# Three edits to a retention and mixer kernel: how late its replay takes a DMA turn to be, which engine turns the third batch's u, and where the first batch's token mixing is added

## The chip, the cores and the metric

The kernel runs on one core of a Trainium2 chip. The metric is the device time of one execution, in microseconds (us). The engines are TensorE (PE in the profile; its weight loads are a row of their own, PEld), VectorE (DVE), ScalarE (ACT), GpSimd (POOL) and SyncE (SP). Each runs its own list of instructions in order and waits for the others through semaphores. Loads of q, k, v and of the weights are issued by POOL, DMA turns (transposes) by SP, stores of the output by ACT.

## What is computed

For 4 batches, 8 heads, 768 steps and head size 64, a decaying state is built up and read at each step, and the result goes through a mixer over tokens and a mixer over channels:

```python
for t in range(S):                                   # gamma = 1 - 2 ** (-5 - h)
    state = gamma * state + einsum('bhd,bhe->bhde', k[:, :, t], v[:, :, t])
    y[:, :, t] = scale * einsum('bhd,bhde->bhe', q[:, :, t], state)
x = y.transpose(0, 2, 1, 3).reshape(B, S, H * D)     # 4 x 768 x 512
h = relu(x^T @ w_tok1) @ w_tok2                      # 768 -> 256 -> 768, over tokens
u = x + h^T
out = u + relu(u @ w_ch1) @ w_ch2                    # 512 -> 1536 -> 512, over channels
```

## The kernel before

The recurrence is done in 6 chunks of 128 steps: within a chunk as a masked score matrix, between chunks through a state that is decayed once per chunk. Work is split into a front and a back.

`front(b, p)` handles one batch b and one pair p of heads (4 pairs, 128 columns of x). In order: k is scaled to fp16 (L408, L410); k and q are turned so that the head size lies on the partitions (kT, qT); the chunk states are formed (L467) and chained on DVE (L476, L479), then scaled (L490, L492); scores are matmuls of kT and qT (L510, two groups of 6), masked by DVE (L518); y is summed from state and scores (L532, L535); ACT or DVE scales it into X (L548, L552); POOL or DVE casts it to fp16 (L565); the first token matrix gives 256 rows (L576), which ReLU copies out as h1 (L584, L586).

Then the batches differ. For **the first batch** u is formed twice. Turned, for the channel mixer's input: L598 multiplies w_tok2 with h1, L601 adds x by an identity matrix, and the sum is copied out as uT (L608). Not turned, for the sum at the end: L627 multiplies h1 with w_tok2 (two groups of 6 matmuls a pair), and DVE adds it to X (L635); these two carry `late=0.5`, so that they stand behind the rest of that batch in priority. For **the other batches** L627 and L635 make u in X, L643 casts it to fp16, and it is turned into uT.

A turn is done in one of two ways. Below batch `XB = 2` TensorE turns k, q and u by 6 or 12 transposing matmuls into a bank (L445, L443, L664), and ACT or DVE copies it out (L452, L670). From batch `XB` on, SP issues a DMA transpose: L431 for k and q, L654 for u.

`back(b)` is the channel mixer, in two halves of 384 tokens. For each of 12 slices of 128 hidden channels 4 matmuls of 384 columns (L696) fill a bank, and ACT copies it out with ReLU into h2 (L710). For each of three blocks of 128 tokens a bank collects 12 matmuls of 512 columns (L723, six pairs); DVE adds X to it (L731), and ACT issues the store (L737).

**Banks.** The accumulator has 8 banks. The first batch's front may use banks 0 to 6, later fronts 0 to 4, every back 5 to 7. A bank is taken by the first matmul into it and is free when its last reader is done.

**The order** is made by the program itself before anything runs. `arrange()` lists operations greedily: of all whose inputs have been placed and for which a bank and buffers are to be had, it looks for those that can start first by its costs, and takes among them (within 20 ns on that engine) the one with the best priority. A front's priority is (0, b, ...), a back's (1, b, number), so a back's work goes where no front's work is ready. `replay(order)` then runs that list against a model of the DMA queues: a DMA starts to move `FIRST` ns after its issue, its rounds take as long as all queues in flight take together, and `LAND` ns later it counts as landed. What the replay gives for each DMA becomes the latency by which the next `arrange()` places it. This is repeated for some turns, and the order with the least replayed time is kept. A matmul that waits on the chip holds up all that stands behind it in TensorE's list. Early in the kernel, matmuls on zeros (L781) fill planned gaps.

The loads form one line on POOL, in order; a load is issued only when the one eight before it has landed. The lines that the prediction speaks of are L431, L510, L576, L598, L601, L608, L627, L635, L654, L664, L670, L696, L710, L723 and the tables in L51 to L79.

Of the kernel before, what the change touches and what calls it, by code (L numbers as in the profile page):

```python
# [17 lines left out]
def kernel(  # L18
# [29 lines left out]
    ctx.enter_context(tc.manual_schedule())  # L48


    BUFS = dict(kf=6, qf=6, k16=3, q16=3, v16=8, kT=4, qT=4, U=2, r16=3, am=8, X=3, x16=5, h1=5, u16=3,  # L51
                uT=3, h2=2, o=4)
    BANKS = dict(first=range(0, 7), front=range(0, 5), back=range(5, 8), fill=range(7, 8))
    SEM = 80
    XB = 2
    ops = []

    class Slot:
# [16 lines left out]
            ops.append(self)  # L75

    GEN = dict(SP=20, ACT=20)
    FIRST = dict(SP=600, POOL=1700, ACT=600)
    LAND = dict(SP=800, POOL=1000, ACT=1500)  # L79

    def replay(order):

        lines = {e: [] for e in ("PE", "ACT", "DVE", "POOL", "SP")}
        held, bank_of = {t: [] for t in BUFS}, {i: None for i in range(8)}
        before = {}
        for o in order:
# [12 lines left out]
        at = {e: 0 for e in lines}  # L99
        free = dict(PE=0, ACT=2500, DVE=0, POOL=400, SP=700)  # L100
        dmas = {e: [] for e in ("SP", "POOL", "ACT")}
        left = {e: None for e in dmas}
        gens = [0, 0, 0]
        t, dt, n = 0, 25, len(order)
        while n:
            for e, line in lines.items():
                while at[e] < len(line) and free[e] <= t:
                    o = line[at[e]]
                    at_ = free[e]
                    for d in o.deps + o.after:  # L110
                        if d.end is None:
                            at_ = None
                            break
                        if d.eng == e and d.eng == "PE":
                            continue
                        at_ = max(at_, d.end + (30 if d.eng == e and not d.dma else SEM))
                    if at_ is None or at_ > t:
                        break
                    for s in before[o]:
                        for u in s.users:  # L120
                            if u.end is None:
                                at_ = None
                                break
                            if u.eng == e and e == "PE":
                                continue
                            at_ = max(at_, u.end + SEM)
                        if at_ is None:
                            break
                    if at_ is None or at_ > t:
                        break  # L130
                    at[e] += 1
                    o.start = at_
                    free[e] = at_ + o.cost[0]
                    if o.dma:
                        if e == "SP":
                            free[e] = max(at_ + 550, gens[-2])
                            gens.append(max(at_ + 550, gens[-1]) + o.dma[0] * GEN[e])
                            o.made = gens[-1]
                        else:
                            o.made = 0  # L140
                        dmas[e].append(o)
                    else:
                        o.end = at_ + o.cost[1]
                        n -= 1
            on = []
            for e, q_ in dmas.items():
                if q_ and left[e] is None and q_[0].start + FIRST[e] <= t:
                    left[e] = float(q_[0].dma[0])
                if left[e] is not None:
                    on.append((e, q_[0]))  # L150
            round_ = sum(o.dma[1] for e, o in on)
            for e, o in on:
                step = dt / round_
                if o.made > t:
                    step = min(step, dt / GEN[e])
                left[e] -= step
                if left[e] <= 0:
                    left[e] = None
                    dmas[e].pop(0)
                    o.end = t + LAND[e]  # L160
                    n -= 1
            t += dt
            if t > 400000:
                raise RuntimeError("the order does not end")
        for o in order:
# [105 lines left out]
    def one(eng, cost, emit):  # L271
        return [(eng, cost[0], cost[1], emit)]
# [79 lines left out]
    loads, x_done, uT_done, y_done, t2_done = {}, {}, {}, {}, {}  # L352
    Xs = [Slot("X") for _ in range(B)]
    UTs = [Slot("uT") for _ in range(B)]
    first_of = {}
    rcount = [0]

    def load(b, p):
# [11 lines left out]
    def front(b, p):  # L370
# [196 lines left out]
            cast_ops.append(op(either(emit, POOL=(460, 530), DVE=(520, 560)),  # L567
                               [ev] + cast_ops, [X16] if hf == 0 else [], [X] if hf == 0 else [X, X16]))

        T1, H1 = Slot(FA), Slot("h1")  # L570

        def emit():
            acc = tile_of(T1, [P, 512], FP)
# [5 lines left out]
                [T1], [X16])  # L579

        def emit(e):
            h1 = tile_of(H1, [P, NJ, P], F16).rearrange("p j c -> p (j c)")
            if e == "ACT":
                nc.scalar.activation(h1, T1.tile[:, :NJ * P], AF.Relu)  # L584
            else:
                nc.vector.tensor_scalar(h1, T1.tile[:, :NJ * P], 0.0, None, ALU.max)  # L586
        hr = op(either(emit, ACT=act(NJ * P), DVE=dve(NJ * P)),
                [t1], [H1], [T1])

        if first:  # L590

            for hf in range(2):
                G = Slot(FA)

                def emit(hf=hf, G=G):
                    acc = tile_of(G, [P, 512], FP)
                    for jt in range(NJ):
                        nc.tensor.matmul(acc[:, :SH], H1.tile[:, jt], wt2[:, jt, hf * SH:(hf + 1) * SH],  # L598
                                         start=(jt == 0), stop=False)
                    for i in range(HC):  # L600
                        nc.tensor.matmul(acc[:, i * P:(i + 1) * P], X16.tile[:, hf * HC + i], ident16,  # L601
                                         start=False, stop=(i == HC - 1))
                g = op(one("PE", (500, 650), emit), [hr, wops["t2"], cast_ops[hf]], [G], [H1, X16])

                def emit(e, hf=hf, G=G):
                    if UT.tile is None:
# [7 lines left out]
                if opens:  # L614
                    first_of[b, "uT"] = e
                uT_done[b, p, hf] = e
        U16 = Slot("u16")
        casts = []
        for hf in range(2):
            T2 = Slot(FA)  # L620

            def emit(hf=hf, T2=T2):
                acc = tile_of(T2, [P, 512], FP)
                for i in range(HC):
                    t = slice((hf * HC + i) * P, (hf * HC + i + 1) * P)
                    for jt in range(NJ):
                        nc.tensor.matmul(acc[:, i * P:(i + 1) * P], wt2[:, jt, t], H1.tile[:, jt],  # L627
                                         start=(jt == 0), stop=(jt == NJ - 1))
            t2 = op(one("PE", (340, 500), emit), [hr, wops["t2"]], [T2], [H1], late=0.5 if first else 0)
            if not first:  # L630
                t2_done[b * NP + p] = t2

            def emit(hf=hf, T2=T2):
                xo = X.tile[:, half(hf), pc]
                nc.vector.tensor_tensor(  # L635
                    xo, xo, T2.tile[:, :HC * P].rearrange("p (i d) -> p i d", d=P), ALU.add)
            ad = op(one("DVE", (500, 560), emit), [t2, cast_ops[hf]], [], [T2, X], late=0.5 if first else 0)
            x_done[b, p, hf] = ad
            if not first:
                def emit(e, hf=hf):  # L640
                    if hf == 0:
                        tile_of(U16, [P, NC, P], F16)
                    (nc.vector if e == "DVE" else nc.gpsimd).tensor_copy(  # L643
                        U16.tile[:, half(hf)], X.tile[:, half(hf), pc])
                casts.append(op(either(emit, POOL=(460, 530), DVE=(520, 560)),
                                [ad] + casts, [U16] if hf == 0 else [], [X] if hf == 0 else [X, U16]))
        if first:
            return
        opens = (b, "uT") not in first_of
        if b >= XB:  # L650
            def emit():
                if UT.tile is None:
                    tile_of(UT, [P, NP, S], F16)
# [25 lines left out]
    def back(b):  # L679
# [6 lines left out]
        for sh in range(2):  # L686
# [28 lines left out]
            for i in range(HC):  # L715
                A, O = Slot("back"), Slot("o")
                last = None
                for f0 in range(0, NF, 2):
                    def emit(f0=f0, i=i, A=A, H2=H2):
                        if f0 == 0:  # L720
                            tile_of(A, [P, 512], FP)
                        for ft in range(f0, f0 + 2):
                            nc.tensor.matmul(A.tile, H2.tile[:, ft, i * P:(i + 1) * P],  # L723
                                             wc2[ft // FW][:, ft % FW],
                                             start=(ft == 0), stop=(ft == NF - 1))
                    last = op(one("PE", (432, 590), emit), rel[f0:f0 + 2] + [wops["c2", f0 // FW], last],
                              [A] if f0 == 0 else [], [H2] if f0 == 0 else [A, H2])

                def emit(sh=sh, i=i, A=A, O=O):
                    o = tile_of(O, [P, C], FP)  # L730
# [29 lines left out]
    for b in range(B):  # L760
        back(b)
    best = None
    for turn in range(10):
        order = arrange()
        t = replay(order)
        if best is None or t < best[0]:
# [47 lines left out]
```

## Time and profile before

| | us |
|---|---|
| median of 3 runs | 220.92 |
| lowest and highest | 220.74, 221.6 |
| the profiled execution | 222.71 |
| its span, first to last instruction | 220.9 |
| TensorE busy | 199.7 |
| ACT, DVE, POOL busy | 110.6, 101.0, 79.3 |
| mean granted clock of TensorE | 0.981 |

The page of the profile gives busy time by engine and by 40 slices of the span, the chain of work that ended last, groups of instructions by line, and DMA issues with the time until they land. Other views show the instructions in order of time, with the idle time of the engine ahead of each and what ended it, the waits by who waited for whom, and busy time and granted clock in chosen stretches. A row such as `L510 PE MATMUL bank<-qT,kT` names the line, the engine, the operation, and what it writes and reads.

### The profile page before, as it was taken

How to read it: one execution, taken by the hardware profiler on the slowest of the kernel's cores; microseconds unless marked ns; L12 is line 12 of the kernel's file. 1: busy time of each engine (PE TensorE's matmuls, PEld its weight loads, DVE VectorE, ACT ScalarE, POOL GpSimd, SP SyncE). 2: the span in 40 equal slices, each digit the busy share in tenths (PEclk: the TensorE clock that was granted, in tenths of full speed). 3: DMA queues.
4: the chain of work that ended last, by engine and by line, in shares of the span. 5: the costliest groups of instructions: out<-in, count | busy, mean ns of one | idle time of the engine just before them, and what ended most of it. 6: DMA issues, size and time to landing. Idle time of an engine off the chain costs nothing.

```text
span 220.9 us, 4774 instructions
## 1 busy us (share of the span) xinstructions
PE 199.7 (90%) x1937; PEld 122.4 (55%) x1937; DVE 101.0 (46%) x272; ACT 110.6 (50%) x237; POOL 79.3 (36%) x113
## 2 busy tenths in 40 slices
PE   7776999999995787767899999999999999999993
PEld 3454687656674465545557666554554645645541
DVE  7387826069995785836477783202103012012021
ACT  3476884758585937806128822550640721712700
POOL 7995943578894554806034113100000000000000
PEclk9999999999999999979699999999999999999998
DMA  7999999999999999999934624302102102112012
GB/s 46 139 157 168 207 207 206 160 156 150 190 166 122 187 155 156 142 176 126 174 105 88 97 48 134 83 0 94 51 0 95 47 3 99 45 47 95 3 47 95
DMA packets 101397, 24.68 MB, mean 112 GB/s; under 512 B 94208, under 2 KB 98304, under 8 KB 101376
## 3 DMA queue, kind: packets, MB, share of 16 engines
q0 software_dynamic: 78720, 13.37, 85.5%
q1 hardware_dynamic: 19200, 4.72, 15.7%
q10 hardware_dynamic: 3456, 6.29, 7.8%
q8 instruction: 15, 0.25, 0.5%
q14 instruction: 6, 0.05, 0.1%
HBM read 26.74 MB, written 6.29 MB: 150 GB/s over the span
## 4 chain that ended last, share of the span: by engine, by line
PE 68%; DMA 17%; POOL 5%; DVE 5%; ACT 2%; issue 1%; ACTq 0%; POOLq 0%; DVEq 0%
PE bank L696 26%; PE bank L723 26%; DMA qT<-q 13%; DMA kf<-in_k_dram 4%; PE bank L627 4%; PE bank L576 3%; PE bank L510 2%; POOL qf L364 2%; POOL v L364 1%; DVE am L518 1%; PE bank L535 1%; PE bank L598 1%; POOL kf L364 1%; PE bank L532 1%; DVE U L479 1%
## 5 line engine op out<-in xcount | busy, mean ns | idle before, releaser
L710 ACT ACTIVATE h<-bank 128x384 f16<-128x384 f32 x96 | 46.4, 491 | 58.1 <-DVE o L731 32.0
L723 PE MATMUL bank<-wc,h 128*128 128x512 f16 x288 | 69.7, 384 | 0.0
L696 PE MATMUL bank<-uT,wc 128*128 128x384 f16 x384 | 68.0, 326 | 0.0
L696 PEld LDWEIGHTS <-wc 128*128 128x128 f16 x384 | 35.8, 98 | 23.4 <-issue 0.4
L731 DVE TENSOR_TENSOR o<-X,bank 128x512 f32<-128x512 f32 x24 | 16.4, 685 | 70.6 <-PE bank L723 70.5
L723 PEld LDWEIGHTS <-h 128*128 128x128 f16 x288 | 26.3, 99 | 27.3 <-issue 0.6
L518 DVE TENSOR_TENSOR am<-bank,mask 128x384 f16<-128x384 f32 x64 | 33.8, 549 | 12.9 <-PE bank L510 12.7
L635 DVE TENSOR_TENSOR X<-X,bank 128x384 f32<-128x384 f32 x32 | 16.4, 549 | 12.3 <-PE bank L627 12.0
L643 POOL CAST u<-X 128x384 f16<-128x384 f32 x22 | 11.0, 514 | 27.8 <-DVE X L635 27.7
L510 PE MATMUL bank<-qT,kT 64*128 64x128 f16 x192 | 10.0, 221 | 11.5 <-DMA qT<-q 11.5
L364 POOL DMA_DIRECT2D qf<-in_q_dram x16 | 16.4, 1023 | 7.0 <-DMA v<-in_v_dram 3.1
L364 POOL DMA_DIRECT2D kf<-in_k_dram x16 | 16.5, 1031 | 5.8 <-DMA wc<-in_moe_w_ch_dram 2.6
L565 POOL CAST x<-X 128x384 f16<-128x384 f32 x27 | 13.6, 517 | 13.4 <-DVE X L552 11.5
L479 DVE SCALAR_TENSOR_TENSOR U<-U,gp,bank 128x64 f32<-128x64 f32 x64 | 17.5, 273 | 0.6
L548 ACT ACTIVATE X<-bank,gy 128x192 f32<-128x192 f32 x42 | 14.9, 420 | 5.6 <-PE bank L535 5.5
L364 POOL DMA_DIRECT2D v<-in_v_dram x16 | 16.4, 1028 | 2.9 <-DMA wc<-in_moe_w_ch_dram 2.4
L408 ACT ACTIVATE k<-kf,gk 128x384 f16<-128x384 f16 x21 | 12.6, 611 | 9.7 <-DMA kf<-in_k_dram 9.6
L510 PEld LDWEIGHTS <-kT 64*128 64x128 f16 x192 | 5.7, 94 | 17.6 <-issue 16.1
L576 PE MATMUL bank<-x,wt 128*128 128x128 f16 x192 | 14.4, 229 | 0.5 <-POOL x L565 0.5
L490 ACT ACTIVATE r<-U 64x320 f16<-64x320 f32 x28 | 13.1, 468 | 3.2 <-DVE U L479 2.8
L576 PEld LDWEIGHTS <-wt 128*128 128x128 f16 x192 | 12.9, 104 | 2.9 <-issue 0.9
L584 ACT ACTIVATE h<-bank 128x256 f16<-128x256 f32 x16 | 6.1, 382 | 16.6 <-PE bank L576 16.6
(58 smaller groups left out, 184.6 us busy)
## 6 DMA issues: line engine op xcount, KB each, us to landing
out_dram<-o ACTq DMA_DIRECT2D x24, 256.0 KB, 2.0
kf<-in_k_dram POOLq DMA_DIRECT2D x16, 192.0 KB, 12.2
qf<-in_q_dram POOLq DMA_DIRECT2D x16, 192.0 KB, 10.9
v<-in_v_dram POOLq DMA_DIRECT2D x16, 192.0 KB, 11.1
wc<-in_moe_w_ch_dram POOLq DMA_DIRECT2D x6, 512.0 KB, 15.5
wt<-in_moe_w_tok_dram POOLq DMA_DIRECT2D x2, 384.0 KB, 9.9
kT<-k SPq DMA_TRANSPOSE x8, 8.1
qT<-q SPq DMA_TRANSPOSE x8, 8.2
```

The costliest lines, as they stand in the source:

```text
L364: nc.gpsimd.dma_start(out=tile_of(s, [P, 2, NC, D], F16), in_=src[b, 2 * p:2 * p + 2].rearrange("h (c p) d -> p (h c) d", p=P))
L479: nc.vector.scalar_tensor_tensor(U[:, c], U[:, c - 1], gp[:, p:p + 1], o, ALU.mult, ALU.add)
L510: nc.tensor.matmul(a[j][:, i], KT.tile[r, t], QT.tile[r, t], start=True, stop=True)
L518: nc.vector.tensor_tensor(am, src, m, ALU.mult)
L548: nc.scalar.mul(X.tile[:, half(hf), h * D:(h + 1) * D], yv[:, :, j * D:(j + 1) * D], gy[:, h:h + 1])
L565: (nc.vector if e == "DVE" else nc.gpsimd).tensor_copy(X16.tile[:, half(hf)], X.tile[:, half(hf), pc])
L576: nc.tensor.matmul(acc[:, jt * P:(jt + 1) * P], wt1[:, i, jt * P:(jt + 1) * P], X16.tile[:, i], start=(i == 0), stop=(i == NC - 1))
L635: nc.vector.tensor_tensor(xo, xo, T2.tile[:, :HC * P].rearrange("p (i d) -> p i d", d=P), ALU.add)
L696: nc.tensor.matmul(acc[:, :SH], w[:, ct, (ft % FW) * P:(ft % FW + 1) * P], UT.tile[:, ct, sh * SH:(sh + 1) * SH], start=(ct == 0), stop=(c ...
L710: nc.scalar.activation(H2.tile[:, ft], A.tile[:, :SH], AF.Relu)
L723: nc.tensor.matmul(A.tile, H2.tile[:, ft, i * P:(i + 1) * P], wc2[ft // FW][:, ft % FW], start=(ft == 0), stop=(ft == NF - 1))
L731: nc.vector.tensor_tensor(o, X.tile[:, sh * HC + i], A.tile, ALU.add)
```

## The change

It has three parts.

The replay's model of turns: `FIRST` for SP goes from 600 to 1150 ns, counted at a quarter of the speed (`BESIDE`) while POOL's queue is moving a load, and a turn's rounds take 12 ns more when another queue moves at the same time. `arrange()` and `replay()` are repeated 16 times instead of 10.

The third batch's u: a new bound `XU = 3` decides for u alone, so that batch 2's u is turned by TensorE (L664, L670 before) and batch 3's still by DMA. k and q of batch 2 stay with DMA.

The first batch's token mixing: its h1 of all four pairs is kept in one constant tile `h1_all` (the pool of h1 buffers shrinks from 5 to 3). L627 and L635 are no longer done for that batch: X keeps x. In place of it each of the six L723 chains of the first batch's back is opened by two matmuls of 512 columns that put h1 times w_tok2 into the chain's bank, for all four pairs at once; the chain adds to it, and L731 adds x. The opener is an operation of its own that takes the bank; it depends on the four h1 and on w_tok2.

```diff
-    BUFS = dict(kf=6, qf=6, k16=3, q16=3, v16=8, kT=4, qT=4, U=2, r16=3, am=8, X=3, x16=5, h1=5, u16=3,
+    BUFS = dict(kf=6, qf=6, k16=3, q16=3, v16=8, kT=4, qT=4, U=2, r16=3, am=8, X=3, x16=5, h1=3, u16=3,
                 uT=3, h2=2, o=4)
-    XB = 2
+    XB, XU = 2, 3
...
-    FIRST = dict(SP=600, POOL=1700, ACT=600)
+    FIRST = dict(SP=1150, POOL=1700, ACT=600)
+    BESIDE = 0.25
...
             for e, q_ in dmas.items():
-                if q_ and left[e] is None and q_[0].start + FIRST[e] <= t:
+                for o in q_:
+                    if o.start < t:
+                        o.seen += dt if e != "SP" or left["POOL"] is None else dt * BESIDE
+                if q_ and left[e] is None and q_[0].seen >= FIRST[e]:
                     left[e] = float(q_[0].dma[0])
...
-            round_ = sum(o.dma[1] for e, o in on)
+            round_ = sum(o.dma[1] for e, o in on) + (12 if len(on) > 1 and left["SP"] is not None else 0)
...
-        T1, H1 = Slot(FA), Slot("h1")
+        T1, H1 = Slot(FA), None if first else Slot("h1")
+
+        def h1_of():
+            return h1_all[:, :, pc] if first else H1.tile
...
+        if first:
+            for hf in range(2):
+                x_done[b, p, hf] = x_ops[hf]
+            return
         U16 = Slot("u16")
...
-        if b >= XB:
+        if b >= XU:
             def emit():
                 if UT.tile is None:
                     tile_of(UT, [P, NP, S], F16)
...
             for i in range(HC):
                 A, O = Slot("back"), Slot("o")
                 last = None
+                if b == 0:
+
+                    def emit(i=i, A=A, sh=sh):
+                        tile_of(A, [P, 512], FP)
+                        t = slice((sh * HC + i) * P, (sh * HC + i + 1) * P)
+                        for jt in range(NJ):
+                            nc.tensor.matmul(A.tile, wt2[:, jt, t], h1_all[:, jt], start=(jt == 0), stop=False)
+                    last = op(one("PE", (432, 590), emit), [h1_done[b, p] for p in range(NP)] + [wops["t2"]], [A])
+                opens = last is None
...
-    for turn in range(10):
+    for turn in range(16):
```

More of the change, by code (lines that the diff above doesn't have):

```diff
@@ L140, in replay @@
                             o.made = 0
+                        o.seen = 0
                         dmas[e].append(o)
@@ L354 @@
     UTs = [Slot("uT") for _ in range(B)]
-    first_of = {}
+    first_of, h1_done = {}, {}
+    h1_all = const_p.tile([P, NJ, C], F16, name="h1_all")
     rcount = [0]
@@ L581, in emit @@
         def emit(e):
-            h1 = tile_of(H1, [P, NJ, P], F16).rearrange("p j c -> p (j c)")
+            if not first:
+                tile_of(H1, [P, NJ, P], F16)
+            t = T1.tile[:, :NJ * P].rearrange("p (j c) -> p j c", c=P)
             if e == "ACT":
-                nc.scalar.activation(h1, T1.tile[:, :NJ * P], AF.Relu)
+                nc.scalar.activation(h1_of(), t, AF.Relu)
             else:
-                nc.vector.tensor_scalar(h1, T1.tile[:, :NJ * P], 0.0, None, ALU.max)
+                nc.vector.tensor_scalar(h1_of(), t, 0.0, None, ALU.max)
         hr = op(either(emit, ACT=act(NJ * P), DVE=dve(NJ * P)),
-                [t1], [H1], [T1])
+                [t1], [] if first else [H1], [T1])
+        h1_done[b, p] = hr
         if first:
@@ L597, in emit @@
                     for jt in range(NJ):
-                        nc.tensor.matmul(acc[:, :SH], H1.tile[:, jt], wt2[:, jt, hf * SH:(hf + 1) * SH],
+                        nc.tensor.matmul(acc[:, :SH], h1_of()[:, jt], wt2[:, jt, hf * SH:(hf + 1) * SH],
                                          start=(jt == 0), stop=False)
@@ L602, in emit @@
                                          start=False, stop=(i == HC - 1))
-                g = op(one("PE", (500, 650), emit), [hr, wops["t2"], cast_ops[hf]], [G], [H1, X16])
+                g = op(one("PE", (500, 650), emit), [hr, wops["t2"], cast_ops[hf]], [G], [X16])
                 def emit(e, hf=hf, G=G):
@@ L628, in emit @@
                                          start=(jt == 0), stop=(jt == NJ - 1))
-            t2 = op(one("PE", (340, 500), emit), [hr, wops["t2"]], [T2], [H1], late=0.5 if first else 0)
-            if not first:
-                t2_done[b * NP + p] = t2
+            t2 = op(one("PE", (340, 500), emit), [hr, wops["t2"]], [T2], [H1])
+            t2_done[b * NP + p] = t2
             def emit(hf=hf, T2=T2):
@@ L636, in emit @@
                     xo, xo, T2.tile[:, :HC * P].rearrange("p (i d) -> p i d", d=P), ALU.add)
-            ad = op(one("DVE", (500, 560), emit), [t2, cast_ops[hf]], [], [T2, X], late=0.5 if first else 0)
+            ad = op(one("DVE", (500, 560), emit), [t2, cast_ops[hf]], [], [T2, X])
             x_done[b, p, hf] = ad
[L639 to L648, printed above, removed]
+            def emit(e, hf=hf):
+                if hf == 0:
+                    tile_of(U16, [P, NC, P], F16)
+                (nc.vector if e == "DVE" else nc.gpsimd).tensor_copy(
+                    U16.tile[:, half(hf)], X.tile[:, half(hf), pc])
+            casts.append(op(either(emit, POOL=(460, 530), DVE=(520, 560)),
+                            [ad] + casts, [U16] if hf == 0 else [], [X] if hf == 0 else [X, U16]))
         opens = (b, "uT") not in first_of
-        if b >= XB:
+        if b >= XU:
             def emit():
@@ L717, in back, with emit @@
                 last = None
+                if b == 0:
[6 more added lines that the diff above has]
+                opens = last is None
                 for f0 in range(0, NF, 2):
-                    def emit(f0=f0, i=i, A=A, H2=H2):
-                        if f0 == 0:
+                    def emit(f0=f0, i=i, A=A, H2=H2, opens=opens):
+                        if f0 == 0 and opens:
                             tile_of(A, [P, 512], FP)
@@ L724, in emit @@
                                              wc2[ft // FW][:, ft % FW],
-                                             start=(ft == 0), stop=(ft == NF - 1))
+                                             start=(opens and ft == 0), stop=(ft == NF - 1))
                     last = op(one("PE", (432, 590), emit), rel[f0:f0 + 2] + [wops["c2", f0 // FW], last],
-                              [A] if f0 == 0 else [], [H2] if f0 == 0 else [A, H2])
+                              [A] if f0 == 0 and opens else [], [H2] if f0 == 0 and opens else [A, H2])
                 def emit(sh=sh, i=i, A=A, O=O):
```

## The prediction

> **What bounds the kernel now.** I read the page's busy line and slices first, then the list of waits, then TensorE's own order of time, the stretches, and last the DMA issues. An engine's name ahead of digits is its busy share in 40 slices of 5.5 us.
>
> ```profile
> span 220.9 us, 4774 instructions
> PE 199.7 (90%) x1937; PEld 122.4 (55%) x1937; DVE 101.0 (46%) x272; ACT 110.6 (50%) x237; POOL 79.3 (36%) x113
> ...
> PE   7776999999995787767899999999999999999993
> ...
> PEclk9999999999999999979699999999999999999998
> ```
>
> TensorE sets the time. From slice 5 on it is full, except in slices 12 to 19 and a little after, 66 to 110 us, where the second and third batches' front stages run. What it waits for there:
>
> ```profile
> PE bank L510 <- DMA qT<-q: 11.5, 5, 3.2
> ```
>
> ```profile
> 70.63 0.34 PE L510 MATMUL bank<-qT,kT 64*128 64x128 f16 x6 [2.21 <-DMA qT<-q]
> ...
> 77.96 0.34 PE L510 MATMUL bank<-qT,kT 64*128 64x128 f16 x6 [2.15 <-DMA qT<-q]
> ...
> 85.08 0.34 PE L510 MATMUL bank<-qT,kT 64*128 64x128 f16 x6 [1.33 <-DMA qT<-q]
> ...
> 95.69 0.34 PE L510 MATMUL bank<-qT,kT 64*128 64x128 f16 x6 [3.23 <-DMA qT<-q]
> ...
> 105.84 0.34 PE L510 MATMUL bank<-qT,kT 64*128 64x128 f16 x6 [2.54 <-DMA qT<-q]
> ```
>
> Five stalls, 2.21 + 2.15 + 1.33 + 3.23 + 2.54 = **11.5 us**, all at the score matmul, all for a q that a DMA turns. PE runs its list in order: the matmuls behind L510, channel-mixer work whose inputs have long been there among them, stand still with it. Two stretches also lost clock (columns: stretch, us, busy of PE, PEld, DVE, ACT, POOL, granted clock, DMA):
>
> ```profile
> 93.00:106.00 13.00, 7.77 (x91) 5.49 (x91) 5.49 (x14) 5.05 (x11) 4.25 (x8) 0.87 1.99 150
> 106.00:116.00 10.00, 10.00 (x97) 6.07 (x94) 6.53 (x16) 1.90 (x5) 1.74 (x4) 0.83 0.77 142
> 116.00:132.00 16.00, 15.96 (x208) 10.93 (x205) 12.35 (x31) 10.71 (x24) 4.26 (x9) 1.00 0.46 80
> ```
>
> 13 x 0.13 + 10 x 0.17 = **3.4 us** of lost clock, right behind the two last stalls. So 14.9 us hang on the turns.
>
> **Why the turns are late, and what the new replay does.** DMA issues between 56 and 106 us, beside the loads, and between 112 and 140 us, after them (last column: us to landing):
>
> ```profile
> kT<-k SPq DMA_TRANSPOSE x6, 8.3
> qT<-q SPq DMA_TRANSPOSE x5, 9.0
> uT<-u SPq DMA_TRANSPOSE x3, 6.2
> ```
>
> ```profile
> uT<-u SPq DMA_TRANSPOSE x5, 2.8
> kT<-k SPq DMA_TRANSPOSE x2, 3.5
> qT<-q SPq DMA_TRANSPOSE x2, 3.0
> ```
>
> A turn beside loads takes 8 to 9 us, one alone about 3. The replay decides which order is kept, and gives the planner the latency that it places by. Its constants before make a turn beside a load 0.6 + 48 x (24 + 13.2 ns) + 0.8 = 3.2 us; after, 1.15 us seen at a quarter of the speed is 4.6, then 48 x (24 + 13.2 + 12 ns) = 2.4, then 0.8: 7.8 us, and about 2.4 more for the second of a pair issued a little over 1 us behind the first, so 8.9. These are the planner's beliefs, not times of the kernel; the trace's 8.3 and 9.0 agree with the new ones and refute the old ones. After 106 us, where the old belief was right, PE lost 0.04 us of the 16 from 116 to 132. So with a true belief PE gets other work ahead of L510. Is there enough? The channel mixer is ready from 35 us for the first batch and has two halves a batch, each as long as
>
> ```profile
> 139.33 7.80 PE bank L696 x48
> 147.13 7.77 PE bank L723 x36
> 154.90 7.80 PE bank L696 x48
> ```
>
> 15.6 us. Five whole halves still stand behind 139.3 us today, so 11.5 us of them can move forward. Bounds for the 14.9: nothing is won, or all. I take all but 2.5 us: one q took longer than the new belief by 11.47 - 8.9 = 2.6.
>
> ```profile
> 94.23 11.47 DMA qT<-q
> ```
>
> [...]
>
> **The third batch's u on TensorE (XU = 3).** SP loses 4 of its 24 turns with their issues; PE gains 4 groups of 6 transposes, and ACT or DVE 4 copies out of a front bank:
>
> ```profile
> 61.05 0.34 PE bank L664 x6
> ```
>
> ```profile
> L670 ACT COPY uT<-bank 128x768 f16<-128x768 f16 x2 | 1.6, 788 | 0.0
> L670 DVE COPY uT<-bank 128x768 f16<-128x768 f16 x2 | 1.1, 544 | 0.0
> ```
>
> PE: 4 x 0.34 = **+1.35 us** on the bounding engine. The copies (2.2 to 3.2 us in all) lie beside matmuls; ACT is 50% busy, DVE 46%. If a copy stood ahead of an L710 or L518 that PE waits for, up to 3.2 us would come back; the range has it. The uT itself is needed first for that batch's L696, at 154.9 us today, so its earlier arrival is worth nothing; k and q of the fourth batch come up in SP's line behind fewer turns, and that gain is inside the 14.9.
>
> **The first batch's token mixing in the mixer's banks.** Removed: 48 matmuls at L627 and 8 adds at L635. Added: 12 matmuls of 512 columns, two ahead of each of six L723 chains.
>
> ```profile
> 31.90 0.34 PE bank L627 x6
> ...
> 33.22 2.35 PE bank L627 x42
> 35.57 7.89 PE bank L696 x48
> 43.46 0.43 PE bank L723 x2
> 43.89 0.34 PE bank L445 x6
> ```
>
> PE: -2.69 + 6 x 0.43 = -0.1 us. The adds:
>
> ```profile
> 33.66 3.34 DVE L635 TENSOR_TENSOR X<-X,bank 128x384 f32<-128x384 f32 x7 [0.77 <-PE bank L627]
> 42.41 0.32 DVE L410 TENSOR_SCALAR k<-kf,gk 128x384 f16<-128x384 f16 x1 [5.41 <-DMA kf<-in_k_dram]
> ```
>
> DVE stands idle for 5.4 us after them until a load lands: worth 0. With that idle gone they would have cost 8 x 0.48 = 3.8.
>
> What costs is **the bank**. The six openers need only h1 and wt2, so the planner sees them ready as soon as the fourth pair's h1 is. Then PE has the last L598/L601 group (the rows above), and after it nothing until uT is copied out:
>
> ```profile
> 32.77 0.97 ACT L608 CAST uT<-bank 128x384 f16<-128x384 f32 x2 [0.35 <-PE bank L601]
> ...
> 35.40 8.05 PE L696 MATMUL bank<-uT,wc 128*128 128x384 f16 x48
> ...
> 36.25 0.49 ACT L710 ACTIVATE h<-bank 128x384 f16<-128x384 f32 x1 [2.52 <-PE bank L696]
> 36.90 0.49 ACT L710 ACTIVATE h<-bank 128x384 f16<-128x384 f32 x1 [0.16 <-PE bank L696]
> ```
>
> Without the six L627 at 31.90, PE is free at 33.22 - 0.34 = 32.88 and uT, whole at 32.77 + 0.97 = 33.74 now, is whole at 33.4: the planner, which takes whatever can start first, puts two openers there (0.86 us, to 33.74). They hold two of the three mixer banks until their six pairs of L723 are done. All of L696 then goes through one bank: matmuls from 35.57 on, 0.66 us a group, then the copy until 36.74, so a cycle from 35.40 to about 36.80, 1.40 us, where now it is 0.66. Behind each L696 that waits stand, in PE's list, the next L723 pairs. From 33.74 to 43.73, where the second batch's first matmul comes, two cycles (2.80 us) hold 1.31 us of L696 and, one pair late, 2 x 0.43 of L723: 10.0 us hold 4.7 + 2.2 = 6.9 us of work, so **+3.1 us** idle, less the 0.1 above. Today that stretch is full:
>
> ```profile
> 33.06:43.73 10.67, 10.67 (x96) 7.24 (x94) 3.66 (x8) 6.62 (x15) 5.05 (x5) 1.00 1.75 184
> ```
>
> Afterwards the second batch's front fills the gaps. Bounds: a free choice of three banks costs +0.9 (0.99 of waiting for uT, which the removed matmuls covered, -0.1); one bank with nothing between costs 12 x (1.40 - 0.66) = +8.9. I take **+3.0**, since held banks' L723 do come ready in pairs. [...]
>
> **Sum.** 220.9 - 11.5 - 3.4 + 2.5 + 1.35 + 3.0 = 212.9. The span is 220.9, the profiled execution 222.71 with 1.8 us around its span, the median of the runs 220.92: the differences are taken off the median, **213.0 us**.
>
> **Rivals.**
> 1. *The openers cost nothing* and all stalls go: 220.9 - 14.9 + 1.35 + 0.9 = 208.3, to 210.5 with 2 us of stalls left. For it: greedy choices hang on 50 ns at the moment when uT comes whole. Against: the 0.5 us of free PE in front of it. 0.14.
> 2. *The next wait takes over*: loads and SP's line stay where they are (the last v is issued at 102.0 us, behind a cast that POOL could start only at 101.56), and half of the 14.9 remains at L467, L510 or L576: 220.9 - 7.4 + 1.35 + 3.0 = 217.9, from 216 to 219.8. Against it: work that waits for no load is there. 0.17.
>
> ```profile
> 101.56 0.51 POOL L565 CAST x<-X 128x384 f16<-128x384 f32 x1 [1.10 <-ACT X L548]
> 102.01 1.01 POOL L364 DMA_DIRECT2D v<-in_v_dram  x1
> ```
>
> 3. *The clock stays down* for a reason other than those waits: 212.9 + 3.4 = 216.3. Both slow stretches begin behind waits of 3.23 and 2.54 us, three shorter ones cost no clock, so 0.05. [...]
> 4. *The order is as before*: best-of-16 on its own replay keeps L510 where it stalls, 220.9 + 1.35 - 0.1 = 222, or 220 with a little won. 0.05.
> 5. *Slower*: openers hold banks in both halves of the first batch's mixer with nothing to fill: 2 x 8.9 = 17.8, so 220.9 - 12.4 + 1.35 + 17.8 = 227.6. It decides from 12 us of bank waits on. For it: three banks only. Against: the second half's openers come behind that half's own L696 in the planner's order. 0.07.
>
> **Chances.** Forecast 0.52, with its own range 210.5 to 216. Slower than 222.0: 0.07 and nothing else; within 0.5% (219.8 to 222.0, what a measurement of this kernel can just tell): 0.05; faster: the rest, 0.88. From 208.5 to 219 about 2 in 10 are left out, on the slow side most.
>
> **What would show it.** Right: L510's waits for qT under 3 us in total, no granted clock under 1.00 from 60 to 130 us, kT and qT still landing in 8 us beside loads; 48 L664 instead of 24; a matmul of h1_all at the new opener ahead of the first L696, the first L710 near 34.6 us, and L710 1.4 us apart until 43 with PE idle for about 3 us. Wrong: openers behind L696 with L710 still 0.65 us apart (rival 1); new waits on loads (rival 2); the five stalls again (rival 4).

## The result, and the profile after

| | before | changed kernel |
|---|---|---|
| median, us | 221.26 (4 runs) | 213.77 (4 runs, 213.17 to 214.35) |
| ratio to before, 95% interval | 1 | **0.967** (0.963 to 0.971) |
| span of the profiled execution, us | 220.9 | 212.6 |
| mean granted clock | 0.981 | 0.992 |

The forecast was 213.0, in a range of 208.5 to 219. The time came out as forecast; two of the terms behind it did not, and their errors, about 3 us each, cancelled.

The lines of the change stand lower in the new kernel: L510 is now L516 (scores), L576 L585, L627 L643, L664 L677 (u turned by TensorE), L670 L683, L696 L709, L710 L723 (ReLU copy of the mixer), L723 L745, and L737 is the new opener.

The page of the changed kernel (span, busy time of the engines, and two rows of the 40 slices):

```profile
span 212.6 us, 4734 instructions
PE 199.1 (94%) x1926; PEld 121.4 (57%) x1926; DVE 97.9 (46%) x267; ACT 112.8 (53%) x244; POOL 77.9 (37%) x111
...
PE   7868899999989999998899999999999999999992
...
PEclk9999999999999999999799999999999999999999
```

TensorE does the same work, 199.1 us against 199.7, in 8.3 us less. The hole between 66 and 110 us has closed but for slices 18 and 19, and one slice has lost clock where two had.

The list of TensorE's waits from 33 us on (us in total, times, longest):

```profile
PE bank L516 <- DMA qT<-q: 2.2, 2, 1.9
PE bank L585 <- POOL x L571: 0.6, 1, 0.6
PE bank L585 <- DVE am L524: 0.5, 1, 0.5
PE bank L516 <- ACT h L595: 0.4, 1, 0.4
```

The waits for a turned q fell from 11.5 to 2.2 us; what is left is nearly all one wait of 1.9. TensorE in order of time, at the first batch's mixer and at that wait:

```profile
32.69 0.59 PE L737 MATMUL bank<-h_all,wt 128*128 128x512 f16 x2
33.12 2.85 PE L709 MATMUL bank<-uT,wc 128*128 128x384 f16 x16
36.04 0.59 PE L745 MATMUL bank<-wc,h 128*128 128x512 f16 x2
36.47 1.46 PE L709 MATMUL bank<-uT,wc 128*128 128x384 f16 x8
...
101.93 0.34 PE L516 MATMUL bank<-qT,kT 64*128 64x128 f16 x6 [1.91 <-DMA qT<-q]
```

One opener, not two, stands ahead of the mixer, which starts at 33.12 instead of 35.40 and runs in groups of four L709 without a pause. Busy time and granted clock (the number behind POOL's) in three stretches:

```profile
33.12:43.40 10.28, 10.21 (x60) 5.66 (x59) 0.32 (x1) 5.99 (x13) 4.62 (x5) 1.00 1.72 184
99.77:103.18 3.41, 1.50 (x26) 1.10 (x24) 0.89 (x2) 0.74 (x3) 0.00 (x0) 1.00 3.12 120
103.18:106.59 3.41, 3.41 (x34) 2.56 (x30) 2.18 (x5) 0.84 (x2) 0.49 (x1) 0.50 2.04 188
```

PE is busy 10.21 of 10.28 us where the forecast had about 3 us idle; and from 103.18 us, shortly behind the wait of 1.91, 3.4 us ran at half clock, a loss of 1.7.

**Where the 8.3 us come from**, span against span:

| | us |
|---|---|
| waits for qT, 11.5 to 2.2 | -9.2 |
| half clock, 3.4 lost to 1.7 lost | -1.7 |
| other short waits of PE behind the first mixer matmul, 0.5 to 1.9 | +1.4 |
| third batch's u on TensorE, 4 groups of 0.34 | +1.35 |
| token mixing: first mixer matmul 2.28 earlier, five more openers of 0.43 later | -0.1 |
| sum | -8.3 |

### The profile page after: what moved, and what is told of

It is laid out like the page before. It is cut to its first block, busy times and chain, and to the rows that moved or that the text cites. A ratio compares the mean times of both kernels' runs of the same rounds, so it can differ in the third digit from the quotient of the medians.

```text
span 212.6 us, 4734 instructions
## 1 busy us (share of the span) xinstructions
PE 199.1 (94%) x1926; PEld 121.4 (57%) x1926; DVE 97.9 (46%) x267; ACT 112.8 (53%) x244; POOL 77.9 (37%) x111
## 4 chain that ended last, share of the span: by engine, by line
PE 58%; DMA 29%; POOL 8%; ACT 2%; issue 2%; DVE 0%; POOLq 0%
PE bank L745 24%; PE bank L709 23%; DMA qT<-q 10%; DMA v<-in_v_dram 8%; DMA wc<-in_moe_w_ch_dram 6%; DMA qf<-in_q_dram 5%; PE bank L643 3%; PE bank L585 3%; POOL kf L370 2%; POOL qf L370 2%; POOL v L370 2%; PE bank L516 2%; PE bank L541 1%; PE bank L538 1%; PE bank L473 1%
## 5 line engine op out<-in xcount | busy, mean ns | idle before, releaser
L723 ACT ACTIVATE h<-bank 128x384 f16<-128x384 f32 x96 | 46.6, 490 | 49.2 <-DVE o L753 32.0
L709 PE MATMUL bank<-uT,wc 128*128 128x384 f16 x384 | 68.8, 328 | 0.0
L745 PE MATMUL bank<-wc,h 128*128 128x512 f16 x288 | 68.5, 379 | 0.1
L709 PEld LDWEIGHTS <-wc 128*128 128x128 f16 x384 | 36.2, 98 | 24.0 <-issue 0.5
L745 PEld LDWEIGHTS <-h 128*128 128x128 f16 x288 | 26.4, 98 | 27.6 <-issue 0.3
L554 ACT ACTIVATE X<-bank,gy 128x192 f32<-128x192 f32 x50 | 17.8, 417 | 9.0 <-PE bank L541 7.5
L658 POOL CAST u<-X 128x384 f16<-128x384 f32 x21 | 10.4, 511 | 24.6 <-DVE X L650 24.6
L571 POOL CAST x<-X 128x384 f16<-128x384 f32 x26 | 12.9, 511 | 12.0 <-ACT X L554 11.9
L650 DVE TENSOR_TENSOR X<-X,bank 128x384 f32<-128x384 f32 x24 | 12.4, 550 | 7.0 <-PE bank L643 6.7
L585 PE MATMUL bank<-x,wt 128*128 128x128 f16 x192 | 13.4, 219 | 1.0 <-POOL x L571 0.6
L541 PE MATMUL bank<-v,am 128*128 128x64 f16 x192 | 13.9, 195 | 0.0
L541 PEld LDWEIGHTS <-am 128*128 128x128 f16 x192 | 12.4, 99 | 1.9
L585 PEld LDWEIGHTS <-wt 128*128 128x128 f16 x192 | 11.6, 98 | 2.9 <-issue 1.1
L803 PE MATMUL bank<-zero 128*128 128x384 f16 x50 | 11.6, 365 | 1.2 <-DVE zero L300 1.2
## 6 DMA issues: line engine op xcount, KB each, us to landing
qf<-in_q_dram POOLq DMA_DIRECT2D x16, 192.0 KB, 11.6
```

Source lines behind the costliest of these rows:

```text
L541: nc.tensor.matmul(o[:, j * D:(j + 1) * D], AM[2 * hf + j].tile[:, i], V.tile[:, j, c], start=(c == 0), stop=(c == 0 or j == 1))
L554: nc.scalar.mul(X.tile[:, half(hf), h * D:(h + 1) * D], yv[:, :, j * D:(j + 1) * D], gy[:, h:h + 1])
L571: (nc.vector if e == "DVE" else nc.gpsimd).tensor_copy(X16.tile[:, half(hf)], X.tile[:, half(hf), pc])
L585: nc.tensor.matmul(acc[:, jt * P:(jt + 1) * P], wt1[:, i, jt * P:(jt + 1) * P], X16.tile[:, i], start=(i == 0), stop=(i == NC - 1))
L709: nc.tensor.matmul(acc[:, :SH], w[:, ct, (ft % FW) * P:(ft % FW + 1) * P], UT.tile[:, ct, sh * SH:(sh + 1) * SH], start=(ct == 0), stop=(c ...
L723: nc.scalar.activation(H2.tile[:, ft], A.tile[:, :SH], AF.Relu)
```

## Experiments

The theory: the gain is the replay's belief about turns; the third batch's u costs its 1.35 us of matmuls, and the token mixing is an even exchange. Rivals: the gain is in the repeats (16 for 10), or in the two other edits; what is left of the waits is loads, clock or stores. The ratios below are to the kernel before, run on the same chip beside each (its median was 221.3 to 223.2 on the chips used, so ratios are compared, not times). Line numbers differ from kernel to kernel: the score matmul is L510, L512, L515 or L516, and a row `bank<-qT,kT` or `DMA qT<-q` is always about it.

### The belief alone, and everything but the belief

The kernel before with only the replay's part of the change (`e1_model_only`), and the changed kernel with that part taken back (`e2_old_model`):

```diff
 # e1: kernel before
-    FIRST = dict(SP=600, POOL=1700, ACT=600)
+    FIRST = dict(SP=1150, POOL=1700, ACT=600)
+    BESIDE = 0.25
...
-    for turn in range(10):
+    for turn in range(16):
 # e2: changed kernel, the same lines the other way round
```

> The kernel before with the replay's new model of turns and its 16 repetitions alone; the third batch's u is still turned by DMA, and the first batch's token mixing is still at L627 and L635. Theory (the gain comes from believing the turns as late as they are): the waits for qT at the score matmul fall from 11.5 us to under 3.5, at most one stretch at half clock is left (1.7 us instead of 3.4), and the time is 220.9 - 11.0 + 1.4 = 211.3 us, between 210 and 214. Rival (the gain comes from the other two edits, fewer turns on SP and a lighter first batch): waits of 8 us or more stay and the time is 218.5 to 222.

> The changed kernel with the old model of turns (600 ns, no slowing beside loads, no 12 ns) and 10 repetitions; the third batch's u on TensorE and the first batch's token mixing in the mixer's banks stay. Theory (late turns): waits for qT of 7 us or more and at least one stretch at half clock, time 218 to 223 us (220.9 + 1.35 - 0.1, less up to 3 us since SP has four turns fewer). Rival (the other two edits carry the gain): waits under 4 us, 212 to 215 us.

Measured: the belief alone 0.965 (0.958 to 0.971), everything but it 0.992 (0.988 to 0.997). The waits of e1, then of e2:

```profile
PE bank L515 <- DMA qT<-q: 3.7, 1, 3.7
```

```profile
PE bank L512 <- DMA qT<-q: 9.6, 4, 3.3
```

The belief, with its 16 repeats, gives the whole ratio of the change (0.967); the repeats are taken apart from it below. One wait of 3.7 us is left, a little more than expected. Without the belief four stalls are back, 9.6 us in all. What the other two edits give without it is 0.8%.

### What two openers ahead of the mixer would have cost

The changed kernel with the first two openers given a priority ahead of the mixer's first matmuls:

```diff
-                    last = op(one("PE", (432, 590), emit), [h1_done[b, p] for p in range(NP)] + [wops["t2"]], [A])
+                    last = op(one("PE", (432, 590), emit), [h1_done[b, p] for p in range(NP)] + [wops["t2"]], [A],
+                              prio=(0, 0, 99) if sh == 0 and i < 2 else None)
```

> The changed kernel with the priority of the first half's first two openers raised, so that both stand ahead of the first L709 and hold two of the three mixer banks; the work is the same. Theory (the prediction's price of one bank): L709's groups are then 1.4 us apart until about 43 us, with the h1-opened chains coming in pairs between them, TensorE is idle for about 3 us more between 33 and 43.5 us than in the changed kernel, and the time is 213.8 + 3 = 216.8 us, between 215 and 219. Rival (a held bank costs nothing here, since the chains fill all gaps): idle under 0.7 us in that stretch, 213 to 215 us.

Measured: 0.981 (0.973 to 0.989), against 0.967. TensorE in order of time:

```profile
32.51 1.03 PE L737 MATMUL bank<-h_all,wt 128*128 128x512 f16 x4
33.37 0.81 PE L709 MATMUL bank<-uT,wc 128*128 128x384 f16 x4
34.76 0.81 PE L709 MATMUL bank<-uT,wc 128*128 128x384 f16 x4 [0.58 <-ACT h L723]
36.15 0.81 PE L709 MATMUL bank<-uT,wc 128*128 128x384 f16 x4 [0.58 <-ACT h L723]
```

and the same stretch as above:

```profile
33.12:43.40 10.28, 7.97 (x46) 4.10 (x44) 0.32 (x1) 4.02 (x9) 4.90 (x5) 1.00 1.74 184
```

With two banks held, a group of L709 starts every 1.39 us, each behind the copy that frees the one bank left, and PE is idle 2.3 of 10.28 us (forecast: 1.40 a group, 3.1 idle by 43.7). So the pitch was right and the idle time a quarter too high; in the changed kernel the price was not charged, because the order has one opener there. The order further on differs too (5.0 us of qT waits here against 2.2), so only the idle time ahead of 43.4 us is the banks'.

### Are the DMA turns beside loads the cause?

The kernel before, with k, q and u of the third batch turned by TensorE instead of DMA:

```diff
-    XB = 2
+    XB = 3
```

> The kernel before with XB = 3: k, q and u of the third batch are turned by TensorE, only the fourth batch's 12 turns stay with DMA; the old model of turns and the old token mixing stay. Theory (DMA turns beside loads are what stalls TensorE, and a turn that is not late cannot): of the five waits for qT the three or four of the third batch go; TensorE gets 4 x (0.34 + 0.46 + 0.34) = 4.6 us more, so 220.9 - 10.6 + 4.6 = 214.9 us, between 213 and 218. Rival (what is late next is the loads, so the waits only change their name): waits of TensorE for loads or casts of 6 us or more between 60 and 106 us, 219 us or more.

Measured: 0.964 (0.958 to 0.970).

```profile
PE bank L510 <- DMA qT<-q: 0.5, 1, 0.5
```

Though the kernel has 164 instructions more in all, and the replay has its old belief, the waits are gone, and with them every stretch of lost clock (mean granted clock 1.00 against 0.981). Four of the five stalls were for q's of the third batch, and those turns are no longer there: take them away, or believe them late, and the ratio is the same. The fifth stall was for a q of the fourth batch. Its turns stay with DMA and are nearly as late as before (8.4 us for qT in the median), yet only 0.5 us is waited for them; why that stall went too is not shown.

### The repeats alone

The kernel before with 16 repeats and nothing else:

```diff
-    for turn in range(10):
+    for turn in range(16):
```

> The kernel before with 16 instead of 10 repetitions of arranging and replaying, and nothing else; the old model of turns stays. Theory (the belief matters, not the search): waits for qT of 8 us or more, time within 1% of before, 219 to 223 us by the first comparison's scale (before 221.3). Rival (the longer search alone finds the better order): waits under 5 us, 217 us or less.

Measured: **1.036** (1.027 to 1.046), slower.

```profile
PE bank L510 <- DMA qT<-q: 13.5, 3, 4.8
```

A time within 1% of before had been expected. The order that was kept has three waits of 4.0 to 4.8 us, and its mean granted clock is 0.955 against 0.981. The search had more orders to choose from, by a model that takes a turn to be 3.2 us, and what it took for the best was worse on the chip. This is one order, and another number of repeats could have drawn a better one. The repeats are not the gain, and e10 below has it with 10 of them.

### The two other edits, undone one at a time

```diff
 # e6: changed kernel
-    XB, XU = 2, 3
+    XB, XU = 2, 2
 # e7: changed kernel with the first batch's token mixing as before (L627, L635 of before; no h1_all, no opener)
```

> The changed kernel with XU = 2: the third batch's u is turned by DMA again; the new model, its repetitions and the first batch's token mixing in the mixer's banks stay. Theory (turning u on TensorE buys nothing, it costs its 1.35 us): waits for qT of 5 us or less, ratio to before 0.955 to 0.972, as the changed kernel's 0.967 or up to 1.35 us better. Rival (four turns fewer on SP are what lets the fourth batch's q land in time): waits of over 5 us, ratio over 0.975.

> The new model with its repetitions and XU = 3, without the third edit: the first batch's token mixing is at L627 and L635 of the kernel before again. Theory (12 matmuls for 48 of a quarter of the width is an even exchange, and one bank held early costs nothing): ratio 0.96 to 0.972, within 1 us of the changed kernel. Rival (the third edit is worth 2 us or more, because the first L696 starts 2.3 us earlier with it): ratio 0.976 or more.

Measured: without the third batch's u on TensorE **0.949** (0.941 to 0.956), with the old token mixing 0.953 (0.946 to 0.961): either is faster than all three edits together, and both lie a little below the ranges expected. Waits of e6, and its busy time in the stretch of the second to fourth fronts, in which the clock is whole:

```profile
PE bank L516 <- DMA qT<-q: 0.8, 1, 0.8
```

```profile
60.00:132.00 72.00, 69.76 (x831) 46.12 (x829) 52.59 (x132) 46.97 (x108) 31.02 (x46) 1.00 1.62 145
```

In e7 the q waits are

```profile
PE bank L515 <- DMA qT<-q: 1.2, 2, 0.9
```

The spans of the changed kernel and e6 differ by 4.7 us: 1.35 of matmuls, 1.7 of clock, and the rest mostly idle time of PE. Only the first can be counted off as the edit's own; the others belong to the order that came out. The four kernels with the new belief show it: the belief with neither edit 0.965, with the token mixing 0.949, with the u 0.953, with both 0.967. Each edit gains when it comes alone (for the u the intervals overlap) and loses when it comes second. A fixed worth of each edit would not change its sign so. Orders differ by that much, about 3 us, as e10 below shows, which has e1's edits and another order. That the order explains all of it is argued and not shown: no run has an edit without the order that comes with it.

### What is left of the waits: an even later belief, and shorter stores

The wait that is left is for a turn that took 11.56 us, from 90.33 on, while three stores of 256 KB, issued at 86, 93 and 99 us, were one after the other in flight. Two tries at it: believe turns still later, or make those stores small. In the second only one row in 128 of the first batch's output is stored (the other rows of that batch are left out); the order is the same.

```diff
 # e8: changed kernel
-    BESIDE = 0.25
+    BESIDE = 0.18
 # e9: changed kernel
-                    nc.scalar.dma_start(out=out[b, t0:t0 + P, :], in_=O.tile)
+                    n = 1 if b == 0 else P
+                    nc.scalar.dma_start(out=out[b, t0:t0 + n, :], in_=O.tile[:n])
```

> The changed kernel with BESIDE = 0.18 instead of 0.25, so that a turn beside loads is believed to take about 1.8 us longer (1.15 / 0.18 = 6.4 instead of 4.6 us ahead of its rounds). Theory (what waits are left come from turns that take longer than even the new belief): the 2.2 us of waits for qT and the stretch at half clock go, 3.9 us less, ratio to before 0.949 to 0.962. Rival (the later belief moves waits to other places, or adds planned gaps): ratio 0.963 or more, with TensorE's other waits over 4 us.

> The changed kernel in its own order, instruction for instruction, but each of the six stores of the first batch moves one row of 512 numbers instead of 128 (the other rows of that batch's output are left out). Theory (the q that took 11.6 us was slow because three stores of that batch were under way beside the loads): that q lands in 9.5 us or less, the wait of 1.91 us for it goes, and so does the stretch at half clock behind it: 3.6 us less than the changed kernel, ratio to before 0.945 to 0.957. Rival (it is slow for the loads and the turns ahead of it alone): 10.5 us or more for that q, a wait of 1 us or more, ratio 0.96 to 0.97.

e8: one of four runs took 211.56 us, the others 215.15 to 215.55, so there is no ratio. The profiled one is one of the longer (215.55), and what follows is seen in it alone. No L516 waits for a q in it. Instead TensorE and ACT, in order of time:

```profile
71.80 1.44 PE L643 MATMUL bank<-h,wt 128*128 128x128 f16 x12 [3.76 <-ACT h L595]
```

```profile
70.51 0.61 ACT L414 ACTIVATE k<-kf,gk 128x384 f16<-128x384 f16 x1 [3.70 <-DMA kf<-in_k_dram]
...
71.39 0.36 ACT L595 ACTIVATE h<-bank 128x256 f16<-128x256 f32 x1
```

ACT stood for 3.70 us before the scaling of a k that had not been loaded; behind it in ACT's list was the ReLU copy that TensorE needed. So in this execution the wait stands at a load instead of a turn; whether it is there in the one of 211.56 us is not known.

e9: 0.946 (0.938 to 0.954), against 0.967. DMA issues between 86 and 106 us (KB each, us to landing) and the time to landing of the three turned q's between 80 and 104, for the changed kernel:

```profile
out_dram<-o ACTq DMA_DIRECT2D x3, 256.0 KB, 8.1
qf<-in_q_dram POOLq DMA_DIRECT2D x2, 192.0 KB, 18.4
```

```profile
DMA to landing us min/median/max: 9.2/9.4/11.6
```

and for e9:

```profile
qf<-in_q_dram POOLq DMA_DIRECT2D x2, 192.0 KB, 11.8
...
out_dram<-o ACTq DMA_DIRECT2D x3, 2.0 KB
```

```profile
DMA to landing us min/median/max: 9.2/9.5/9.9
```

```profile
PE bank L516 <- DMA qT<-q: 1.9, 2, 1.1
```

The slowest turn is 9.9 instead of 11.6 us, and the wait of 1.91 and the half clock behind it are gone (granted clock 1.00 from 99 to 107 us). The waits for q's have hardly fallen in all (1.9 for 2.2): two shorter ones, of 1.1 and 0.8 us, stand elsewhere and cost no clock. (The profiled execution of e9 lost clock between 17.7 and 24.6 us, 0.51 in the mean, ahead of all these stores.) So the stores made that turn late; whether directly or by way of the loads, which landed sooner too (11.8 for 18.4), this run doesn't tell apart. Nor are stores all that can make a turn so late: the q of 11.47 us in the kernel before had one store issued between 86 and 106 us, and three turns of u.

### Does the replay pick the best of its orders?

The same edits with another number of repeats. Each kernel keeps the order that its replay takes to be the shortest, so fewer repeats can only keep one that it holds to be no better.

```diff
 # e10: e1,  e11: changed kernel
-    for turn in range(16):
+    for turn in range(10):
 # e12: e6
-    for turn in range(16):
+    for turn in range(24):
```

> The kernel with the new model of turns alone, as the run with only the model, but with 10 repetitions, so that another order of nearly the same replayed time is kept. Theory (with the right belief the orders differ by a few us through single waits that the replay does not see, and the one wait of 3.7 us with its half clock was such a draw): waits for qT anywhere from 0 to 4 us, time within 5 us of that run either way, ratio 0.945 to 0.975, and clearly below 0.99. Rival (the 16 repetitions are part of the gain): ratio over 0.98.

> The changed kernel with 10 repetitions instead of 16, and nothing else. By the replay's own account its order is 3.9 us worse than the changed kernel's. Theory (the replay ranks such orders no better than by a few us): ratio 0.945 to 0.98 to before, on either side of the changed kernel's 0.967. Rival (the replay ranks well): 3 to 5 us slower than the changed kernel, ratio 0.98 to 0.99.

> The changed kernel with XU = 2 and 24 repetitions, the order that the replay likes best for these edits, by 1.7 us over the one of the run without the third batch's u on TensorE. If the replay ranks well: 1 to 2 us faster than that run, ratio 0.94 to 0.946. Theory (it ranks no better than by a few us): ratio 0.942 to 0.965, and it may as well be slower than that run's 0.9485.

Measured: e10 0.949 (0.942 to 0.955) where 16 repeats gave 0.965; e11 0.954 (0.947 to 0.960) where 16 gave 0.967; e12 **0.944** (0.937 to 0.952) where 16 gave 0.949. Waits of the three:

```profile
PE bank L515 <- DMA qT<-q: 2.0, 2, 1.4
```

```profile
PE bank L516 <- DMA qT<-q: 1.9, 3, 0.7
```

```profile
PE bank L516 <- DMA qT<-q: 1.2, 2, 1.0
```

Orders that the replay holds to be no better were faster on the chip twice, outside the intervals. In e10 and e11 the longest q wait is 1.4 and 0.7 us, in their kernels with 16 repeats 3.7 and 1.9. The new belief keeps the replay from orders with five stalls, but does not tell orders apart that differ by one. The fastest kernels that compute the whole output are e12, e6 and e10, at 0.944 to 0.949 with overlapping intervals. e10 has the new belief alone. So neither of the two other edits is shown to be worth anything: with the belief and a good order, the kernel is as fast without them.

## Why the prediction was right, and where it was not

**The cause and its size.** Right: "So 14.9 us hang on the turns", and a true belief moves mixer work ahead of the score matmul. The turns still take as long beside loads (8.6 us for kT, 9.4 for qT between 56 and 102 us, in the issue view), so it is the order that changed and not the turns.

**What is left of the stalls: mis-sized.** The step "I take all but 2.5 us" came out as 5.3. Its reason was right: one q took longer than the new belief, 11.56 us against 8.9. But the term had only that wait in it. Measured are 2.2 us of q waits, 1.7 of clock behind the longest of them, which the prediction counted as gone, and 1.4 of short waits that the new order adds.

**The third batch's u.** +1.35 as forecast: 48 L677 for 24, and no row of TensorE's waits names the copies (changed kernel, by line):

```profile
L677 PE MATMUL bank<-ident,u 128*128 128x128 f16 x48 | 4.0, 219 | 0.0
L683 ACT COPY uT<-bank 128x768 f16<-128x768 f16 x6 | 4.8, 793 | 2.4 <-PE bank L677 2.4
```

**The bank: the step that failed.** The prediction says that the planner "puts two openers there (0.86 us, to 33.74)", and one opener is there. It took it that PE has nothing else to do from 32.88 until the whole uT is there at 33.4, so that a second opener could start at 33.31. But the code asks only for `uT_done[b, p, sh]`, the copies of the first half. In the changed kernel ACT makes the last two copies, one of each half, from 32.40 to 33.37, and the mixer starts at 33.12, behind the first of the two and ahead of the end of the second:

```profile
32.40 0.97 ACT L620 CAST uT<-bank 128x384 f16<-128x384 f32 x2 [0.18 <-PE bank L613]
```

So the gap held one opener, two of three banks stayed free, and the term was 0 instead of +3.0. e3 shows that with the second opener the price is near what was worked out (1.39 us a group for 1.40, 2.3 us idle for 3.1). The lower bound of +0.9 was wrong too: the exchange of 48 matmuls and 8 adds for 12 matmuls of 512 columns gave -0.1, since the mixer began as soon as the one opener was done.

**The sum.** 2.8 us too little for the stalls and 3.1 too much for the bank: 212.9 forecast for the span, 212.6 measured. That the sum came within 0.3 us is luck: the two errors cancelled. That most of the 14.9 us was won is not. With the bank's term mended and the 2.5 kept the sum would have been 209.8, within rival 1's band, and 3 us too little for the changed kernel.

**The rivals.** Rival 1 was right about the openers (0.64 us between copies, not 1.4) but not about the stalls. Rival 2, the next wait takes over, did not happen here; the profiled execution of e8 has it in a place that the rival did not name, a load ahead of ACT's copy. Rival 3 falls: e4, e6 and e7, whose longest q waits are 0.5, 0.8 and 0.9 us, have a granted clock of 1.00 from 60 to 132 us. Rivals 4 and 5 did not come.

**The signs named.** Right: q waits under 3 us, turns as slow as before, 48 L677, an opener ahead of the mixer. Wrong: no lost clock from 60 to 130 us (one stretch), the first copy near 34.6 us (it starts at 33.98), copies 1.4 us apart with 3 us idle.

## What to carry to other kernels

Where an order is planned ahead, put into the model the latency that the trace shows for each transfer in the company in which it runs; more search with a wrong latency made this kernel 3.6% slower in the one case run. Once the model is right, edits of 1 us cannot be judged by one order each, since orders that differ by one wait are 3 us apart: undo each edit alone, and time the orders that the model ranks next. Here the belief alone, with another order, came out as fast as the best of the kernels with more edits. And before pricing a wait for a whole buffer, look in the code for how much of it the waiting instruction really needs.

## What the runs showed of the hardware

**In these runs a longer wait did not always lose more clock.** TensorE's waits for a q in four runs (us, and the time at which the score matmul behind each starts), and the granted clock there:

| run | wait | granted clock |
|---|---|---|
| kernel before | 2.21 at 70.63, 2.15 at 77.96, 1.33 at 85.08 | 1.00 from 65.85 to 96.56 |
| kernel before | 3.23 at 95.69, 2.54 at 105.84 | 0.50 from 96.56 to 99.97 and from 106.80 to 110.21 |
| changed kernel | 1.91 at 101.93 | 0.50 from 103.18 to 106.59 |
| e2 | 2.62 at 70.75, 1.79 at 76.71, 1.96 at 87.23 | 1.00 from 66.09 to 100.22 |
| e2 | 3.27 at 102.50 | 0.50 from 103.64 to 107.05 |
| e5 | 4.01 at 70.85 | 0.50 from 69.21 to 76.04 |

Behind the wait of 3.23 us in the kernel before (first PE's busy time, the granted clock behind POOL's):

```profile
96.56:99.97 3.41, 3.41 (x30) 2.66 (x30) 2.17 (x6) 0.00 (x0) 0.53 (x2) 0.50 1.80 193
```

Around the wait of 2.62 us in e2, where the clock stays whole:

```profile
66.09:69.50 3.41, 2.04 (x28) 1.08 (x25) 2.39 (x6) 3.12 (x8) 2.81 (x4) 1.00 1.70 152
69.50:72.91 3.41, 2.12 (x36) 1.60 (x37) 1.80 (x6) 0.30 (x2) 0.00 (x0) 1.00 2.03 157
```

And at the wait of 4.01 us in e5, where 6.83 us ran at half clock, a loss of 3.4:

```profile
69.21:72.62 3.41, 1.77 (x11) 0.92 (x12) 0.56 (x1) 0.24 (x1) 1.00 (x1) 0.50 1.93 193
72.63:76.04 3.41, 3.41 (x42) 2.98 (x40) 1.96 (x5) 1.38 (x4) 1.52 (x3) 0.50 1.58 165
```

So the wait of 1.91 us in the changed kernel had 1.7 us of lost clock behind it, and the one of 2.62 us in e2 had none. No run was made to tell what decides between them.
